# Program order on every engine, paired inverse-RMS chains and step-paced loads in a windowed-attention and feed-forward kernel

## The chip, the cores and the metric

One core of one Trainium2 chip. The metric is device time of one execution in microseconds (us), lower is better. The clock that the throttle grants to the matmul engine is recorded for each run.

Engine names are those of the profile: PE (TensorE, matmul), PEld (its weight loads), DVE (VectorE), ACT (ScalarE), POOL (GpSimd), SP (SyncE, which here only issues DMAs).

## The reference

Two stages, cut to what matters. Attention over 4 batches, 8 heads, 768 tokens, head size 64, where a token sees 128 earlier tokens and the first 4 ("sinks"). Its output, 3072 tokens of 512 values, goes through RMS normalization and a SwiGLU feed-forward network (FFN) with 1536 hidden values.

```python
keep = is_sink | in_window                       # window 128, 4 sinks
a = softmax(where(keep, q @ k.T / 8, -1e9));  x = a @ v        # per head
x = x.transpose(0, 2, 1, 3).reshape(3072, 512)
xn = x / sqrt(mean(x * x) + 1e-6) * rms_g
g = xn @ w_gate
out = (g * sigmoid(g) * (xn @ w_val)) @ w_out
```

## The kernel before

The work is cut into 24 attention blocks of 128 tokens (6 a batch) and 6 FFN groups of 4 blocks (512 tokens). While PE runs the FFN of group G, the attention of the blocks of group G+1 and later is woven in between.

The names that the profile uses: `qs`, `ks`, `v` are loaded blocks; `qkT` the transposed q and k; `pT` scores in PSUM; `et` their exponentials; `pv` attention output with its denominator; `x` the normalized attention output; `sq` and `ms` its squares and their sums; `m`, `y` the inverse-RMS chain; `xr` the RMS-normalized block; `pxt` and `xnt` its transpose in PSUM and SBUF (blocks 8 and later are transposed by DMA); `pg`, `pvl` gate and value matmuls; `th`, `p`, `hT` the three steps of SwiGLU; `po` output matmuls; `osb` their eviction.

The inverse RMS of one block, on DVE, six small dependent operations and then `xr`:

```python
def unit_rms(g):
    x16 = X16.pop(g).rearrange("p h d -> p (h d)")
    ms = MS.pop(g)
    nc.vector.scalar_tensor_tensor(out=m, in0=ms[:, 0:1], scalar=RMS_EPS, in1=ms[:, 1:2], ...)
    nc.vector.tensor_scalar(out=y[:, 0:1].bitcast(I32), in0=m.bitcast(I32), ...)   # first guess
    # ... four more scalar_tensor_tensor on [128, 1] ...
    # unit_xr:
    nc.vector.scalar_tensor_tensor(out=xr, in0=x16, scalar=y[:, 4:5], in1=gb, ...) # times rms_g
```

The FFN is a list of "parts". For each hidden tile `ft` there is a gate part and a value part; for each of the four token blocks three output parts, each of which contracts four of the twelve hidden tiles:

```python
def gate():
    st["pg"] = mms("pg", wg, G, fts, cols)                       # PE, 4 matmuls 128x512
    nc.scalar.activation(out=st["th"], in_=st["pg"], func=Tanh)  # ACT
def val():
    pvl = mms("pvl", wv, G, fts, cols)
    nc.vector.scalar_tensor_tensor(out=p1, in0=st["th"], in1=st["pg"], ...)   # DVE: p
    nc.vector.tensor_tensor(out=HT[...], in0=p1, in1=pvl, op=mult)            # DVE: hT
def part(i):                                                     # output part i of 3
    for ft in range(4 * i, 4 * i + 4):
        nc.tensor.matmul(out=st["po"], lhsT=HT[(G, ft // 2)][...], rhs=wo[:, ft, :], ...)
```

Attention units are put in "slots", four for each step, and `weave` spreads the slots evenly over the parts. Which engines keep this order is said by the schedule context:

```python
MANUAL = {PE, SP}
MANUAL_ALL = MANUAL | {Activation, DVE}
with tc.manual_schedule(engines=MANUAL_ALL):     # start: blocks 0 and 1
    unit_warm(6)                                 # dummy matmuls
    # ...
with tc.manual_schedule(engines=MANUAL):         # main part
    for ft in range(0, FA, 2):                   # FA = 10: five tile pairs in token halves
        fa += parts_f(0, (ft, ft + 1), slice(0, GN // 2))
        fb += parts_f(0, (ft, ft + 1), slice(GN // 2, GN))
    # ...
    for G in range(NG):
        # ... gate/value parts, then the output parts of the group
        weave(parts, slots[n:n1], 1)
```

An engine in the set keeps program order; for the others the scheduler picks the order when the program is built. In the main part of this kernel ACT and DVE are left to the scheduler. The token halves of the first group let its FFN start when only blocks 0 and 1 are ready.

The softmax here doesn't subtract the row's maximum and nothing guards it: scores larger than these inputs give would overflow.

## Time and profile before

| | before |
|---|---|
| median time, three executions | 255.85 us (255.73 to 256.4) |
| PE busy | 240.8 us, 95% |
| first FFN matmul | 19.39 us |
| second group starts | 76.43 us |
| PE waits after the first FFN matmul | nine, 5.7 us together |

The page of the kernel before: busy time by engine, then rows of 40 equal slices of the span, where a digit is the busy share in tenths (`PEclk` is the granted clock in tenths).

```profile
PE 240.8 (95%) x1784; PEld 125.2 (49%) x1784; DVE 175.7 (69%) x465; ACT 141.9 (56%) x320; POOL 94.8 (37%) x127
...
PE   6988899989979999999999999999999999999994
...
DVE  4563897998768999348898277998268991277800
...
PEclk9979999999999999999999999999999999999999
```

PE has nines from about 80 us on; all of its waits but one (0.40 us at 128.6 us) lie in front. Busy times in stretches of 10 us, of the kernel before. The columns are stretch, length, then PE, PEld, DVE, ACT and POOL with instruction counts, granted clock, DMA, GB/s:

```profile
40.00:50.00 10.00, 9.50 (x116) 7.76 (x115) 8.96 (x25) 8.32 (x18) 4.64 (x6) 1.00 1.51 195
50.00:60.00 10.00, 9.02 (x92) 5.50 (x93) 9.71 (x26) 8.51 (x21) 9.76 (x12) 1.00 2.43 156
60.00:70.00 10.00, 9.61 (x106) 5.81 (x106) 7.83 (x26) 9.32 (x23) 9.98 (x12) 1.00 2.32 173
...
140.00:150.00 10.00, 10.00 (x69) 4.78 (x67) 3.92 (x14) 5.25 (x14) 0.00 (x0) 1.00 0.34 92
```

From 40 to 70 us DVE and ACT are nearly as full as PE. Who waited for whom on PE, kernel before (us in total, times, longest):

```profile
PE pg L582 <- ACT xnt L568: 1.8, 2, 1.6
PE pT L405 <- ACT qkT L274: 1.4, 2, 1.0
...
PE pv L439 <- DVE hT L608: 0.4, 1, 0.4
```

This is the end of the second group on DVE, kernel before, in order of time (start, duration, engine, line, operation):

```profile
98.35 0.16 DVE L526 SCALAR_TENSOR_TENSOR y<-y 128x1 f32<-128x1 f32 x1
98.42 0.68 DVE L600 SCALAR_TENSOR_TENSOR p<-th,pg 128x512 bf16<-128x512 bf16 x1
99.02 0.75 DVE L542 SCALAR_TENSOR_TENSOR xr<-x,y,gb 128x512 bf16<-128x512 bf16 x1
99.68 0.68 DVE L608 TENSOR_TENSOR hT<-p,pvl 128x512 bf16<-128x512 bf16 x1
...
101.07 0.69 DVE L608 TENSOR_TENSOR hT<-p,pvl 128x512 bf16<-128x512 bf16 x1
```

### The profile page before, as it was taken

To read this page: it belongs to the slowest core of one execution; us is meant where nothing else is said; L and a number is where in the kernel's file an instruction comes from. 1 tells how busy PE (TensorE), PEld (TensorE's weight loads), DVE (VectorE), ACT (ScalarE), POOL (GpSimd) and SP (SyncE) were. 2 spreads that over 40 slices of the span, in tenths; PEclk is the share of its full clock that TensorE was granted. 3 is DMA by queue.
4 is the path that set the end of the run, shared out by engine and by line. 5 is a ranking of instruction groups with operands and counts; after the bars stand their busy time and mean duration, and the time that the engine had idled before them with its cause. 6 is when DMAs were issued, how large, how long until landed. Compare 5 with 4: busy or idle time off the path is not lost.

```text
span 254.6 us, 4880 instructions
## 1 busy us (share of the span) xinstructions
PE 240.8 (95%) x1784; PEld 125.2 (49%) x1784; DVE 175.7 (69%) x465; ACT 141.9 (56%) x320; POOL 94.8 (37%) x127
## 2 busy tenths in 40 slices
PE   6988899989979999999999999999999999999994
PEld 2536677755534444454454444444444444444441
DVE  4563897998768999348898277998268991277800
ACT  2646678879994565475475366566445341333211
POOL 8986778299987440331231003033121000000000
PEclk9979999999999999999999999999999999999999
DMA  9999999999999999435005328215321101200022
GB/s 130 142 171 190 188 157 189 183 156 155 185 174 168 156 155 118 97 89 147 10 12 64 82 62 147 41 23 64 104 61 45 21 18 63 107 0 0 3 82 82
DMA packets 105849, 25.74 MB, mean 101 GB/s; under 512 B 95073, under 2 KB 102753, under 8 KB 105826
## 3 DMA queue, kind: packets, MB, share of 16 engines
q0 software_dynamic: 80704, 13.90, 70.6%
q1 hardware_dynamic: 24082, 11.28, 20.0%
q10 hardware_dynamic: 1040, 0.26, 0.5%
q8 instruction: 14, 0.23, 0.4%
q14 instruction: 9, 0.07, 0.1%
HBM read 28.31 MB, written 6.29 MB: 136 GB/s over the span
## 4 chain that ended last, share of the span: by engine, by line
PE 68%; DVE 12%; ACT 8%; POOL 4%; DMA 3%; issue 2%; POOLq 0%; DVEq 0%; ACTq 0%
PE po L623 20%; PE pg L582 20%; PE pvl L582 19%; DVE hT L608 3%; DVE p L600 3%; DMA ks<-in_k_dram 3%; PE pT L405 2%; ACT et L414 2%; DVE et L380 2%; ACT sq L495 2%; PE pv L453 2%; PE pv L457 2%; ACT qkT L274 1%; DVE x L485 1%; POOL qs L111 1%
## 5 line engine op out<-in xcount | busy, mean ns | idle before, releaser
L582 PE MATMUL pg<-xnt,wg 128*128 128x512 bf16 (+1 forms) x328 | 74.0, 353 | 2.3 <-ACT xnt L568 1.8
L582 PE MATMUL pvl<-xnt,wv 128*128 128x512 bf16 (+1 forms) x328 | 74.0, 353 | 0.0
L595 ACT ACTIVATE th<-pg 128x512 bf16<-128x512 f32 x72 | 43.2, 600 | 51.2 <-PE pg L582 49.8
L623 PE MATMUL po<-wo,hT 128*128 128x512 bf16 x288 | 64.9, 379 | 0.1
L600 DVE SCALAR_TENSOR_TENSOR p<-th,pg 128x512 bf16<-128x512 bf16 x72 | 49.2, 683 | 18.9 <-ACT th L595 18.9
L608 DVE TENSOR_TENSOR hT<-p,pvl 128x512 bf16<-128x512 bf16 x72 | 49.4, 686 | 5.7 <-PE pvl L582 0.9
L582 PEld LDWEIGHTS <-wg 128*128 128x128 bf16 x328 | 31.4, 98 | 30.9 <-issue 2.7
L582 PEld LDWEIGHTS <-wv 128*128 128x128 bf16 x328 | 31.2, 98 | 28.8 <-issue 0.2
L414 ACT ACTIVATE et<-pT 128x512 bf16<-128x512 f32 x76 | 39.5, 605 | 6.7 <-PE pT L405 6.7
L623 PEld LDWEIGHTS <-hT 128*128 128x128 bf16 x288 | 27.4, 98 | 30.6 <-issue 0.2
L382 POOL TENSOR_SCALAR_AFFINE_SELECT et<-et 128x512 bf16<-128x512 bf16 x20 | 12.6, 637 | 79.7 <-ACT et L414 73.2
L630 ACT ACTIVATE osb<-po 128x512 f32<-128x512 f32 x24 | 14.4, 601 | 27.8 <-PE po L623 25.4
L495 ACT ACTIVATE sq<-x 128x256 bf16<-128x256 bf16 x48 | 20.2, 425 | 7.5 <-DVE x L485 7.1
L111 POOL DMA_DIRECT2D qs<-in_q_dram x23 | 20.9, 907 | 7.0 <-DMA wo<-in_moe_w_out_dram 2.5
L111 POOL DMA_DIRECT2D ks<-in_k_dram x23 | 20.8, 904 | 6.6 <-DMA wo<-in_moe_w_out_dram 2.9
L124 POOL DMA_DIRECT2D v<-in_v_dram x24 | 21.7, 903 | 4.3 <-DMA qs<-in_q_dram 2.7
L485 DVE TENSOR_TENSOR x<-pv,rden 128x256 bf16<-128x256 f32 x48 | 20.0, 422 | 0.9
L380 DVE TENSOR_TENSOR et<-et,masks 128x1024 bf16<-128x1024 bf16 (+1 forms) x22 | 13.9, 636 | 8.5 <-ACT et L414 8.4
L542 DVE SCALAR_TENSOR_TENSOR xr<-x,y,gb 128x512 bf16<-128x512 bf16 (+1 forms) x25 | 18.1, 728 | 0.7
L480 DVE RECIPROCAL rden<-pv 128x4 f32<-128x4 f32 x48 | 7.8, 173 | 10.1 <-PE pv L457 10.0
L405 PE MATMUL pT<-qkT 64*128 64x256 bf16 (+1 forms) x168 | 12.0, 261 | 2.1 <-ACT qkT L274 1.4
L457 PE MATMUL pv<-v,et 128*128 128x65 bf16 x168 | 12.6, 194 | 0.0
(72 smaller groups left out, 198.3 us busy)
## 6 DMA issues: line engine op xcount, KB each, us to landing
out_dram<-osb SPq DMA_DIRECT2D x24, 256.0 KB, 2.2
v<-in_v_dram POOLq DMA_DIRECT2D x24, 128.0 KB, 7.6
qs<-in_q_dram POOLq DMA_DIRECT2D x23, 128.0 KB, 7.5
ks<-in_k_dram POOLq DMA_DIRECT2D x23, 128.0 KB, 7.5
wg<-in_moe_w_gate_dram POOLq DMA_DIRECT2D x6, 256.0 KB, 8.6
wv<-in_moe_w_val_dram POOLq DMA_DIRECT2D x6, 256.0 KB, 8.9
wo<-in_moe_w_out_dram POOLq DMA_DIRECT2D x2, 768.0 KB, 10.7
osb<-in_k_dram ACTq DMA_DIRECT2D x1, 256.0 KB, 4.5
```

Of the source, the lines that this page charges most:

```text
L111: nc.gpsimd.dma_start(out=tl, in_=src[b, :, t * P:(t + 1) * P, :].rearrange("h t d -> t h d"),)
L124: nc.gpsimd.dma_start(out=V16[b][:, t, :, 0:D], in_=v[b, :, t * P:(t + 1) * P, :].rearrange("h t d -> t h d"),)
L380: nc.vector.tensor_tensor(out=e, in0=e, in1=mv, op=ALU.mult)
L414: nc.scalar.activation(out=et[:, hi].rearrange("p j n c -> p (j n c)"), in_=banks[u][hi], func=ACT.Exp, scale=inv_sqrt_d,)
L485: nc.vector.tensor_tensor(out=X16[g][:, heads_of(g, u), :], in0=pvv[:, :, 0:D], in1=RDEN.pop((g, u)).unsqueeze(2).to_broadcast((P, 4, D)), ...
L495: nc.scalar.activation(out=sq, in_=xh, func=ACT.Square, scale=MS_SCALE, accum_out=MS[g][:, u:u + 1],)
L542: nc.vector.scalar_tensor_tensor(out=XR[g][-1], in0=x16[:, c], scalar=y[:, 4:5], in1=gb[:, c], op0=ALU.mult, op1=ALU.mult,)
L582: nc.tensor.matmul(out=ps[:, i * n:(i + 1) * n], lhsT=w_sb[:, kt, ft * P:(ft + 1) * P], rhs=XNT[G][:, kt, cols], start=(kt == 0), stop=(kt ...
L595: nc.scalar.activation(out=st["th"], in_=st["pg"], func=ACT.Tanh, scale=0.5)
L600: nc.vector.scalar_tensor_tensor(out=p1, in0=st["th"], scalar=1.0, in1=st["pg"], op0=ALU.add, op1=ALU.mult,)
L608: nc.vector.tensor_tensor(out=HT[key][:, i:i + n, cols], in0=p1.rearrange("p (n c) -> p n c", n=n), in1=pvl.rearrange("p (n c) -> p n c", ...
L623: nc.tensor.matmul(out=st["po"], lhsT=HT[(G, ft // 2)][:, ft % 2, tb * P:(tb + 1) * P], rhs=wo[:, ft, :], start=(ft == 0), stop=(ft == FTN ...
```

## The change

Its intent: take the scheduler's guesses out of the main part and place everything by hand; save DVE work by sharing one RMS chain between two blocks; start the FFN sooner; and spread the loads so that masks can move to POOL. The diff, cut to its core (cuts marked with `# ...`):

```diff
-    FA = 10
-    POOL_MASK_FROM = 2
-    MANUAL = {mybir.EngineType.PE, mybir.EngineType.SP}
+    FA = 8
+    POOL_MASK_FROM = 1
+    MANUAL = {mybir.EngineType.PE, mybir.EngineType.SP, mybir.EngineType.Pool}
# ... loads: no longer all at once behind the output weights, but by step
+    LOADS = {4: (8, 9), 5: (10, 11), 6: (12,), 7: (13, 14), 8: (15,), ...}
# ... blocks 12 and 18 are transposed by DMA too
-        return g >= DMA_T_FROM and g % NT > 0
+        return g >= DMA_T_FROM
# ... work put off by n parts
+    def later(n, f):
+        if DEFER[0] and n:
+            LATER.append([n, f])
+        else:
+            f()
+    def tick():                       # after each part
+        for e in LATER:
+            e[0] -= 1
+        # ... runs what is due
+            wait = 0 if not dve else 1 if g < GB else 1 + 2 * u      # masks on DVE
+                later(wait, lambda u=u, et=et, his=his: masked(u, et, his))
-            unit_sq(g, u)
-        if u == 1 and g >= 2:
-            unit_rms(g)
+            later(1 if g < GB else 2, lambda: unit_sq(g, u))
+        if u == 1 and g >= 2 and g % 2 == 1:
+            later(2 if g < GB else 4, lambda: unit_rms(g))           # both blocks of a pair
# ... unit_rms: seven operations on [128, 2], then xr of both blocks in a row
+        for i in range(2):
+            unit_xr(g - 1 + i, y[:, 5, i:i + 1])
# ... blocks 0 to 3: xr without rms_g, which the transposed eviction applies
+            nc.vector.tensor_scalar(out=xr, in0=x16, scalar1=y, scalar2=None, op0=ALU.mult)
# ... start: 9 warm-up matmuls, not 6, and others moved
-    with tc.manual_schedule(engines=MANUAL):
+    with tc.manual_schedule(engines=MANUAL_ALL):
+        DEFER[0] = True
+        run(fa, [ ... ])
+        run(fb[:8], [
+            [unit_bias(3, 1), unit_x(2), unit_sp(3, 1), unit_x(3)],
# ...
```

## The prediction

> **What bounds the kernel now.** TensorE (PE). The page gives PE 95% busy, and from 80 us on the timeline shows feed-forward (FFN) matmuls back to back: four 128x512 in 0.86 us. Stretch by stretch, PE is busy 10.0 of 10 us nearly everywhere after 80 us, but 7.5 to 9.6 before. So what can be won lies in the first 80 us:
> - The first FFN matmul starts at 19.39 us.
> - After it the timeline shows nine PE waits, together 5.7 us: 0.74 on ACT qkT, 0.74 on DVE qkT, 0.50 and 0.40 for DVE, 0.98 and 0.39 on ACT qkT, 0.17 and 0.23 around xnt, and 1.59 on ACT xnt before the second FFN group at 76.4. With about 0.17 us of modelled matmul tail before each, my estimate is 7.3 us.
> - From 40 to 70 us DVE is busy 7.8 to 9.7 of 10 us and ACT 8.3 to 9.3; their queues cause those waits.
>
> **What the change does.**
> 1. Two blocks share one inverse-RMS chain. Now each block pays six dependent DVE operations, 13.28 to 14.47 us for the first. Two chains become one of seven (estimate 1.35 us). For the first four blocks the gain moves to the transposed eviction, so xr should cost about 0.3 us (as masks, 128x512, 0.29), not 0.75. Both first xr should be ready at 15.8 us, not 17.1, and no 2.3 us of warm-up matmuls stand between the two transposes. First FFN matmul: about 18.2 us, gain 1.2.
> 2. Blocks 12 and 18 are transposed by DMA: 16 fewer PE transposes, 0.44 us a block, gain 0.9 us of bound PE time.
> 3. Masks of blocks 7 to 11 move from DVE (two of 0.69 us) to POOL (four of 0.64). DVE gets slack. POOL issues loads too (0.9 us each), so it becomes nearly full about 57 to 73 us.
> 4. Program order on ACT, DVE and POOL, with masks, squares and RMS put off by one to four parts, and the last x transposes of the second group placed ahead of four or more output matmuls: this should remove most of the 0.98, 0.50 and 1.59 us waits; gain about 3.2 us after 38 us.
> 5. Four tile pairs in halves, not five: the same matmul time, but the second half of the tokens is needed 1.7 us of PE work earlier. I expect a new wait: the transposes of blocks 2 and 3 stand right before the matmuls that need them, with two exps (1.0 us) between their evictions on ACT. Estimate 2.3 us against 0.75 now, loss 1.5; about 1.2 us is won back before it.
>
> Loads land in about 7.5 us; two blocks ahead should suffice. Nothing changes after 130 us.
>
> **Sum.** 1.2 + 0.9 + 3.2 + 1.2 - 1.5 = 5.0 us; perhaps more, since the tuning removes waits that I only guessed. Predicted 250.6 us, 80% range 247.5 to 253.8. Chances: faster by over 2% 0.50, within 2% 0.47, slower 0.03.
>
> **What would show it.** First FFN matmul near 18.2 us (right) or after 19 (step 1 wrong). DVE below 8 of 10 us in 40 to 70. Second FFN group starting about 72 us with no wait on xnt. A wait of 1 to 2.5 us on xnt or xr near 34 us (step 5). Sixteen fewer 128x128 PE transposes.
>
> **What would make it wrong.** Masks on POOL late behind load issues. ACT blocked at the head of its queue by program order. PE at half speed in the first FFN matmuls: the Trainium skill ("TensorE: Matmul & The Clock Gate", The HAM clock gate) tells of a half-rate clock after low activity; this trace agrees, warm-ups taking 0.47 us each at 16 to 18 us against 0.22 at full speed.

## More of the kernel before

The scheduler threaded an RMS chain between `p` and `hT`, a small operation at a time, and the last `hT` is done at 101.8 us. On PE the output matmuls start at 101.02 us, and the twelfth, the first to need that `hT`, comes over 2 us later, so it doesn't wait:

```profile
101.02 1.89 PE L623 MATMUL po<-wo,hT 128*128 128x512 bf16 x8
...
103.00 3.18 PE L623 MATMUL po<-wo,hT 128*128 128x512 bf16 x14
```

## The result and the profile after

| | before | after |
|---|---|---|
| median time, four executions of each | 255.79 us (255.45 to 256.4) | 264.62 us (264.12 to 267.6) |
| first FFN matmul | 19.39 us | 17.09 us |
| second group starts | 76.43 us | 75.97 us |
| third group starts | 112.99 us | 118.21 us |
| sixth group starts | 219.7 us | 230.3 us |
| span of the profiled run | 254.6 us | 265.6 us |

The ratio is 1.036 (95% interval 1.030 to 1.043): slower, where 0.98 was expected. Ratios here are the mean time of one kernel's fast runs over that of the other's of the same rounds, so they are not quite the ratio of the medians that are quoted. The milestones are those of the profiled runs. After the change the attention work of one step (8 `pT`, 18 `pv` and 4 `pss` matmuls, about 1.3 us of PE time) has moved from before the second group's start to behind it, so 75.97 us is about 0.8 us later than 76.43 us for the same work (estimate). From the third group's start on, both kernels have done the same attention work.

The page of the changed kernel, same rows as before:

```profile
PE 244.9 (92%) x1735; PEld 124.3 (47%) x1761; DVE 167.9 (63%) x398; ACT 139.0 (52%) x322; POOL 106.1 (40%) x145
...
PE   7989879998999996999998998998999998999993
...
DVE  4644757796658988317979139988139984078700
...
PEclk9968979999999999799999999999999999999998
```

DVE has less to do (167.9 against 175.7 us), as intended, and PE is idle more. There are new gaps far behind 80 us, once in each group, and dips of the clock near 18, 37 and 109 us. Stretches of the changed kernel:

```profile
40.00:50.00 10.00, 9.95 (x105) 7.13 (x103) 7.21 (x13) 6.81 (x13) 5.61 (x7) 1.00 1.50 191
...
60.00:70.00 10.00, 8.66 (x86) 4.97 (x86) 5.55 (x18) 9.61 (x25) 9.32 (x12) 1.00 1.24 99
...
100.00:110.00 10.00, 7.58 (x41) 3.24 (x41) 7.59 (x21) 4.20 (x12) 1.86 (x4) 0.86 0.94 82
...
140.00:150.00 10.00, 8.69 (x62) 4.10 (x61) 6.83 (x18) 3.68 (x9) 1.47 (x3) 1.00 0.30 41
```

PE's waits in the changed kernel:

```profile
PE po L669 <- DVE hT L654: 6.0, 4, 2.2
...
PE pg L628 <- ACT xnt L617: 1.2, 1, 1.2
PE pxt L601 <- DVE xr L574: 1.1, 1, 1.1
```

The new first line is the largest. The four waits are at 106.0, 146.3, 185.1 and 222.4 us, one at the end of each group from the second to the fifth. The first of them on PE:

```profile
101.27 2.54 PE L669 MATMUL po<-wo,hT 128*128 128x512 bf16 x11
106.00 0.39 PE L669 MATMUL po<-wo,hT 128*128 128x512 bf16 x1 [2.20 <-DVE hT L654]
```

Eleven output matmuls run, and the twelfth, the one that needs tile 11, waits. On DVE at that time:

```profile
100.69 0.69 DVE L654 TENSOR_TENSOR hT<-p,pvl 128x512 bf16<-128x512 bf16 x1
101.30 0.68 DVE L409 TENSOR_TENSOR et<-et,masks 128x1024 bf16<-128x1024 bf16 x1
101.90 0.15 DVE L541 SCALAR_TENSOR_TENSOR m<-ms 128x2 f32<-128x2 f32 x1
...
103.14 1.42 DVE L578 SCALAR_TENSOR_TENSOR xr<-x,y,gb 128x512 bf16<-128x512 bf16 x2
104.47 0.68 DVE L646 SCALAR_TENSOR_TENSOR p<-th,pg 128x512 bf16<-128x512 bf16 x1
105.26 0.69 DVE L654 TENSOR_TENSOR hT<-p,pvl 128x512 bf16<-128x512 bf16 x1
```

A mask and the whole paired RMS chain with both `xr`, from 101.90 to 104.47 us, stand ahead of the last `p` and `hT`. Nothing needs that `xr` soon: the third group starts at 118 us. The operation that PE needs is last in the queue. The Trainium skill ("TensorE: Matmul & The Clock Gate", Architectural detail) says of the queues that "ACT/DVE are strict FIFO"; this trace agrees: the inputs of the last `p` and `hT` were there by about 101.4 us (ACT's last `th` and PE's last `pvl` matmul are done by then), yet DVE first works off 2.6 us of RMS, and PE stands 2.2 us until the two operations behind it are done.

The wait that the prediction had foreseen where the token halves meet, on PE:

```profile
33.86 0.40 PE L601 MATMUL pxt<-ident,xr 128*128 128x128 bf16 x4 [1.15 <-DVE xr L574]
...
36.10 1.91 PE L628 MATMUL pg<-xnt,wg 128*128 128x256 bf16 x8 [1.17 <-ACT xnt L617]
37.80 1.58 PE L628 MATMUL pvl<-xnt,wv 128*128 128x256 bf16 x8
39.22 1.04 PE L628 MATMUL pg<-xnt,wg 128*128 128x256 bf16 x8
```

1.15 and 1.17 us. After it eight matmuls take 1.70 us to the next group's start (36.10 to 37.80), where they take 0.87 us elsewhere: PE runs at half rate. The granted clock in three stretches of the changed kernel (the clock is the number before the last two):

```profile
14.00:22.00 8.00, 7.14 (x51) 4.48 (x50) 3.09 (x8) 4.00 (x11) 6.17 (x9) 0.57 1.87 179
34.00:40.00 6.00, 4.83 (x40) 3.44 (x39) 3.24 (x7) 2.71 (x7) 5.45 (x7) 0.72 2.49 155
104.00:112.00 8.00, 5.78 (x38) 2.73 (x40) 3.90 (x10) 4.12 (x12) 3.86 (x6) 0.79 0.53 100
```

It is 0.57, 0.72 and 0.79. In the kernel before the same stretches have 0.79, 1.00 and 1.00. Over the runs of the changed kernel the mean clock was 0.993 to 0.972 and the time 264.12 to 267.6 us, in the main the slower the lower, so these dips go with up to 3.5 us from run to run; the best-clocked run is still 8 us over before.

### The profile page after: what moved, and what is told of

Read it like the earlier page. It is cut to its first block, busy times and chain, and to the rows that moved or that the text cites. A ratio compares the mean times of both kernels' runs of the same rounds, so it can differ in the third digit from the quotient of the medians.

```text
span 265.6 us, 4787 instructions
## 1 busy us (share of the span) xinstructions
PE 244.9 (92%) x1735; PEld 124.3 (47%) x1761; DVE 167.9 (63%) x398; ACT 139.0 (52%) x322; POOL 106.1 (40%) x145
## 4 chain that ended last, share of the span: by engine, by line
PE 58%; DVE 28%; ACT 8%; issue 4%; DMA 1%; DVEq 0%; ACTq 0%
PE po L669 17%; PE pg L628 16%; PE pvl L628 15%; DVE hT L654 7%; DVE p L646 6%; DVE xr L578 5%; ACT et L443 2%; PE pT L434 2%; ACT th L641 2%; DVE x L522 2%; PE pqk L241 2%; DVE et L409 2%; DMA osb<-in_q_dram 1%; PE pv L487 1%; PE pv L483 1%
## 5 line engine op out<-in xcount | busy, mean ns | idle before, releaser
L628 PE MATMUL pg<-xnt,wg 128*128 128x512 bf16 (+1 forms) x310 | 75.2, 364 | 3.2 <-ACT xnt L617 1.2
L669 PE MATMUL po<-wo,hT 128*128 128x512 bf16 x279 | 66.5, 385 | 6.6 <-DVE hT L654 6.0
L411 POOL TENSOR_SCALAR_AFFINE_SELECT et<-et 128x512 bf16<-128x512 bf16 x30 | 19.5, 656 | 85.8 <-ACT et L443 77.9
L669 PEld LDWEIGHTS <-hT 128*128 128x128 bf16 x288 | 27.7, 99 | 39.3 <-DVE hT L654 8.0
L517 DVE RECIPROCAL rden<-pv 128x4 f32<-128x4 f32 x48 | 8.4, 176 | 32.5 <-PE pv L487 32.5
L416 POOL TENSOR_SCALAR_AFFINE_SELECT et<-et 128x512 bf16<-128x512 bf16 x24 | 16.0, 667 | 0.0
L578 DVE SCALAR_TENSOR_TENSOR xr<-x,y,gb 128x512 bf16<-128x512 bf16 x20 | 14.9, 785 | 0.4
## 6 DMA issues: line engine op xcount, KB each, us to landing
out_dram<-osb SPq DMA_DIRECT2D x24, 256.0 KB, 2.2
wg<-in_moe_w_gate_dram POOLq DMA_DIRECT2D x6, 256.0 KB, 8.1
wv<-in_moe_w_val_dram POOLq DMA_DIRECT2D x6, 256.0 KB, 8.2
osb<-in_q_dram SPq DMA_DIRECT2D x1, 256.0 KB, 3.9
```

Source lines behind the costliest of these rows:

```text
L411: nc.gpsimd.affine_select(out=ev[:, :, 0, :], in_=ev[:, :, 0, :], compare_op=ALU.is_ge, fill=0.0, base=0, pattern=[[0, x], [1, P]], channe ...
L578: nc.vector.scalar_tensor_tensor(out=xr, in0=x16, scalar=y, in1=gb, op0=ALU.mult, op1=ALU.mult,)
L628: nc.tensor.matmul(out=ps[:, i * n:(i + 1) * n], lhsT=w_sb[:, kt, ft * P:(ft + 1) * P], rhs=XNT[G][:, kt, cols], start=(kt == 0), stop=(kt ...
L669: nc.tensor.matmul(out=st["po"], lhsT=HT[(G, ft // 2)][:, ft % 2, tb * P:(tb + 1) * P], rhs=wo[:, ft, :], start=(ft == 0), stop=(ft == FTN ...
```

## The experiments

Fifteen kernels, all correct. Unless said otherwise a time is the median of all runs (in e1, e2, e12 and e13 one of them is marked slow), and "before" in the same rounds had 255.5 to 256.0 us.

A run is marked slow when it is over 1.5% above the fastest of its kernel; ratios use the other, fast runs alone. Theory A was: program order on DVE (and ACT) in the main part costs the time, because the RMS chain stands ahead of the last `hT`. Rival B: the paced loads and the masks on POOL. Rival C: the half-rate clock.

### e1 and e2: give the order back to the scheduler

```diff
-    with tc.manual_schedule(engines=MANUAL_ALL):      # main part
+    with tc.manual_schedule(engines=MANUAL):          # e1: ACT and DVE free
+    with tc.manual_schedule(engines=MANUAL | {Activation}):   # e2: DVE free
```

> The changed kernel with ScalarE and VectorE left to the scheduler again in the main part, as before; all else of the change stays. Theory A (program order on these two engines lost the time, chiefly the four waits of the output matmuls for hT, 1.25 to 2.2 us each): those four waits go, and the time falls by 6 us or more, to 258 us or less. Rival B (the loads and the masks on GpSimd cost it): the time stays within 2 us of 264.5. Rival C (the half-rate clock after the early start costs it): the time falls by under 3 us.

> Only VectorE is left to the scheduler; ScalarE keeps program order. Theory A with VectorE as the culprit: within 1 us of e1_free, 258 us or less. If program order of ScalarE matters as much: about half of e1_free's gain. Rivals B and C: near 264.5 us.

Measured: e1 268.95 us (ratio 1.050), e2 266.81 us (1.040). Neither gains; e1 is even slower. The waits of `po` for `hT` do shrink (to 1.3 and 1.0 us), but another takes their place. PE's waits in e1:

```profile
PE pg L628 <- ACT xnt L608: 4.7, 1, 4.7
PE pxt L601 <- DVE xr L574: 2.5, 3, 2.1
```

On DVE in e1:

```profile
75.16 0.35 DVE L296 COPY ksk<-qkT 64x16 bf16<-64x16 bf16 x2 [3.32 <-DMA qkT<-ks]
```

The RMS of blocks 6 and 7 is not late: both `xr` are done at 71.8 us and their transposes on PE at 72.3. But `ksk`, DVE's copy of the next batch's sink keys, waits until 75.16 us for a DMA transpose of 6.1 us (block 12, which step 2 of the prediction took off PE). The normalization `x` of the next block stands behind it on DVE, the squares of `x` stand ahead of the last `xnt` on ACT, and the second group starts 4.7 us late (4.2 us in e2, by the same chain). So the blunt form of theory A, "program order is bad here", falls: the scheduler's order of this program is no better. What matters is where single operations stand. That the scheduler would do better with block 12 still transposed on PE was not tried.

### e3: move one pair of operations

From block 8 on the RMS chain is put off by six parts, not four. On DVE this moves only `p` and `hT` of one tile ahead of each chain; PE, ACT and POOL keep the same order instruction for instruction (SP's DMA issues shift with it).

```diff
-            later(2 if g < GB else 4, lambda: unit_rms(g))
+            later(2 if g < GB else 4 if g < DMA_X_FROM else 6, lambda: unit_rms(g))
```

> Program order kept on every engine; from block 8 on the inverse RMS of a pair is put off by six parts, not four, which moves only the last p and hT of each group ahead of it on VectorE (TensorE, ScalarE and GpSimd have the same order). Theory A in its sharp form (the 2.7 us RMS chain ahead of the last hT): the waits of po for hT fall from 6.0 us in total to under 1, and the time falls by about 6 us, with the clock dip near 107 us gone too, to 257 to 259 us. Rival B or C: no change, 264 us.

Measured: 257.66 us (256.76 to 258.28), ratio to before 1.007. Of the 8.8 us, 7.0 us are gone (264.62 less 257.66). The same place on PE in e3:

```profile
100.43 2.75 PE L669 MATMUL po<-wo,hT 128*128 128x512 bf16 x12
103.11 0.61 PE L434 MATMUL pT<-qkT 64*128 64x256 bf16 x8
```

All twelve output matmuls run through. And on DVE in e3:

```profile
101.06 0.68 DVE L646 SCALAR_TENSOR_TENSOR p<-th,pg 128x512 bf16<-128x512 bf16 x1
101.85 0.69 DVE L654 TENSOR_TENSOR hT<-p,pvl 128x512 bf16<-128x512 bf16 x1
102.45 0.15 DVE L541 SCALAR_TENSOR_TENSOR m<-ms 128x2 f32<-128x2 f32 x1
...
103.70 1.42 DVE L578 SCALAR_TENSOR_TENSOR xr<-x,y,gb 128x512 bf16<-128x512 bf16 x2
```

`hT` first, the RMS chain after it. No wait of `po` for `hT` is left, and the clock in the stretch 104 to 112 us is 1.00. The waits were 6.0 us, or 6.7 with about 0.17 us of matmul tail hidden before each (an estimate). The clock has a share in the 7.0 us: runs with the same mean clock took 264.12 us (changed kernel, 0.993) and 258.10 and 258.28 us (e3, 0.992 and 0.993), so about 5.9 us are the order itself and about 1 us goes with the lower clock of the other runs of the change. This is the sharp form of theory A, and it is shown. It also speaks against C as the main cause: in e3's profile the clock dip at 34 to 40 us is still there (0.74).

### e4: program order alone, in the kernel before

```diff
-    with tc.manual_schedule(engines=MANUAL):          # main part of before
+    with tc.manual_schedule(engines=MANUAL_ALL):
```

> The kernel before, with program order on ScalarE and VectorE in the main part and nothing else. If program order as such costs the time, with no deferral to soften it: 262 to 275 us, with waits on hT and on masks. If only the change's own deferral did it: within 2 us of 255.8.

Measured: 275.19 us, ratio 1.075. PE waits for `xnt`, `qkT` and `ksk` again and again up to 90 us, and the second group starts at 88.9 us. Program order without any put-off is worse than the change by 10 us. That the deferral makes this difference is argued, for the change differs from e4 in its start, its paired chains, its loads and its masks too.

### e7: the old loads and masks (rival B)

On top of e3, all loads at once behind the output weights, and masks of blocks 7 to 11 back on DVE.

```diff
-    POOL_MASK_FROM = 1
+    POOL_MASK_FROM = 2
-        load_q(2 * GB)
-    LOADS = {4: (8, 9), 5: (10, 11), ...}
+    LOADS = {}
+        for g in range(2 * GB, NB):       # ahead of the main part
+            unit_load(g)
```

> e3_rms_late with the loads and the masks of the kernel before: all loads issued at once after the output weights, masks of blocks 7 to 11 on VectorE. Rival B (the new loads and masks cost time): the time falls by over 2 us, to 255.5 or less. If they help, as the prediction said, by unloading VectorE: the time rises, by 1 to 6 us. If they don't matter: 257 to 258.5.

Measured: 256.71 us (255.89 to 257.17), ratio 1.004 against e3's 1.007, with overlapping intervals. That is below the 257 to 258.5 us expected if they don't matter and above the 255.5 of rival B, and within the noise of e3. Rival B falls as the cause of the 8.8 us, and so does my hope that they help: loads and masks together are worth nothing that shows (e11 against e10, below, says the same).

### e5 and e8: undo the four-pair split, first try

Five pairs again, and the transposes of blocks 2 and 3 one part ahead of their reader. e5 on top of e3, e8 on the changed kernel as it is.

```diff
-    FA = 8
+    FA = 10
-        run(fa, [
+        run(fa[:8], [
# ... in run(fb[:8], ...) the first slot becomes empty
-            [unit_bias(3, 1), unit_x(2), unit_sp(3, 1), unit_x(3)],
+        run(fa[8:], [
+            [],
+            [unit_bias(3, 1), unit_x(2), unit_sp(3, 1), unit_x(3)],
```

> e3_rms_late plus the undoing of the four-pair split: five tile pairs in halves again, and the transposes of blocks 2 and 3 one part ahead of the first matmul that needs them. If step 5 of the prediction is right (the split costs a wait of 1.1 us on xr and 1.2 us on xnt near 32 to 34 us, and the half-rate clock that follows it costs some 1.5 us more): those waits fall below 0.5 us together, the clock dip at 34 to 37 us goes, and the time falls by 2.5 to 3.5 us from 257.7, to 254 to 255. If the split is innocent: 257 to 258 us.

> The changed kernel with only that last edit (five pairs, transposes one part earlier), the RMS chain left where the change put it. If the two causes add: 264.6 less about 3, so 261 to 262 us, with the four waits for hT still there (5 to 7 us in total). If the time gained in front only lengthens the waits for hT: 263.5 us or more.

Measured: e5: three of its four runs were marked slow (its profiled run had a clock of 0.842 and took 292 us), and the one fast run took 260.98 us. e8: 274.26 us, ratio 1.073, 10 us slower than the change. The two waits where the halves meet did fall, from 1.15 and 1.17 to 0.58 and 0.20 us. PE's largest waits in e8:

```profile
PE pxt L601 <- DVE xr L578: 8.1, 2, 4.4
PE po L669 <- DVE hT L654: 6.0, 4, 2.2
```

The edit had a flaw. The rest of the first group now has 18 parts, not 20, for the same slots, so fewer parts lie between an attention block and the transposes of its pair. The chains of blocks 4 and 5 and of blocks 6 and 7, put off by four parts, came to stand right ahead of their readers. A delay counted in parts is tied to how many parts a group has. A second thing made it worse. The first operation of the chain on DVE in e8:

```profile
57.41 2.65 DVE L541 SCALAR_TENSOR_TENSOR m<-ms 128x2 f32<-128x2 f32 x1
```

Where no mask ran on POOL at the time, it took 0.15 to 0.16 us. Here four masks ran back to back on POOL from 57.65 to 60.04 us, and it ended at 60.06.

### e6: e5 with two more edits

In each step the transposes of a coming block ahead of the x transposes, and the second mask one part sooner.

```diff
-            wait = 0 if not dve else 1 if g < GB else 1 + 2 * u
+            wait = 0 if not dve else 1 if g < GB else 1 + u
# step(): slots[1].append(unit_t(g + 2)) now comes before unit_x
```

> e5_fa10, and in each step the transposes of a coming block issued ahead of the x transposes (against the 1.0 us wait of the sink scores on ScalarE's qkT near 63 us and the 0.4 us on xnt before the second group), and the second mask of a block one part earlier. If the remaining loss is these waits: 252 to 253.5 us, faster than before by about 1%. If VectorE has no room in the first 100 us: within 1 us of e5_fa10.

Measured: 264.87 us, ratio 1.035. The 1.0 us wait of the sink scores is gone, but it carries the flaw of e5 (waits of 2.9 and 3.8 us for `xr`), so as an attempt at a better kernel it says little.

### e9, e10 and e11: the same without the flaw

```diff
-            later(1 if g < GB else 2, lambda: unit_sq(g, u))
-            later(2 if g < GB else 4 if g < DMA_X_FROM else 6, lambda: unit_rms(g))
+            later(1 if g < DMA_X_FROM else 2, lambda: unit_sq(g, u))
+            later(2 if g < DMA_X_FROM else 6, lambda: unit_rms(g))
# e10: e9, and unit_t(g + 2) before unit_x within a step
# e11: e10, and loads and masks as in e7
```

> e5_fa10 again without its flaw: the parts of the first group got fewer, so a delay counted in parts put the RMS chain of blocks 4 to 7 right before its reader; here squares and RMS of these blocks are put off by one and two parts, not two and four. If the four-pair split and that flaw are separate causes: no wait on xr above 0.5 us at blocks 4 and 6, and 253.5 to 255.5 us, some 3 us under e3_rms_late. If five pairs do not fit program order at all: 258 us or more.

> e9_fa10_soon with the transposes of a coming block ahead of the x transposes within a step. If the 1.0 us wait of the sink scores on ScalarE's qkT near 62 us still binds, it goes and the time falls by about 1 us; if it has slack already, no change within 0.7 us.

> e10_tfirst with the loads and masks of the kernel before. e7_old_loads was 1 us under e3_rms_late, within the noise of either. If that was real: 1 us under e10_tfirst, and about 252 to 254 us, below the kernel before by 0.5 to 1.5%. If it was noise, or VectorE has less room here: equal to e10_tfirst or up to 2 us above.

Measured: e9 256.54 us (ratio 1.003), e10 257.03 (1.004), e11 256.98 (1.005). e9 is 1.1 us under e3, not 3. The waits where the halves meet are 0.28 and 0.20 us, down from 2.3, and the clock stays at 1.00 from 20 to 110 us; but a wait of 1.88 us appears at 57 us, attention on the mask of block 6, and 0.74 us on `xr` at 69 us. In e10 and e11 the sink scores no longer wait, and DVE's masks cost PE 3.2 and 4.5 us (2.6 in e9). Much of what one edit wins in the first group, the next wait in it takes back, but not all. The profiled runs show where the rest goes. In e9 the second group starts at 72.68 us, 3.75 us before that of the kernel before; 1.3 us of this is the work moved behind it, so about 2.4 us are won (estimate). The second group then takes 38.80 us against 36.56, with the moved work and with waits of 0.49 and 0.33 us for `hT` and `p` at 93 us. The fourth takes 37.81 us against 36.62, with waits of 0.40 and 0.78 us near 158 us. PE's last matmul ends only 0.6 us earlier than before.

### e12, e13 and e14: what is left

```diff
# e12: e9, DVE free in the main part
# e13: e9, both masks of blocks 4 to 6 put off by one part
-            wait = 0 if not dve else 1 if g < GB else 1 + 2 * u
+            wait = 0 if not dve else 1 if g < DMA_X_FROM else 1 + 2 * u
# e14: e13, and from block 8 on the two xr each a part later than the chain
-            unit_xr(g - 1 + i, y[:, 5, i:i + 1])
+            later(0 if g < DMA_X_FROM else 1 + i,
+                  lambda i=i: unit_xr(g - 1 + i, y[:, 5, i:i + 1]))
```

> e9_fa10_soon with VectorE left to the scheduler in the main part. If program order on VectorE is what keeps the repaired change above the kernel before: the waits on hT, p and et after 90 us go and the time falls to 253 to 255. If the scheduler's order is no better for this program, as e1 and e2 (269 and 267 us) suggest: 258 us or more, with a new wait on xr or xnt before the second group.

> e9_fa10_soon with both masks of blocks 4 to 6 put off by one part instead of one and three. If the late second mask is a cause of its own: the wait of the attention matmuls on et near 57 us (1.9 us) goes and the time falls by 1 to 2 us, to 254.5 to 255.5. If VectorE merely passes the delay on (to xr, hT or rden): within 0.7 us of e9's 256.5.

> e13_mask_soon with the RMS chain of blocks 8 on cut in three on VectorE: the chain, then one xr, then the other, each a part later, so that no block of 2.7 us stands in VectorE's queue. If long solid blocks in an in-order queue are the cause of what remains after 75 us (waits on p and hT of 0.3 to 0.8 us, two or three in a group): those waits at least halve and the time falls by 1 to 2 us under e13, to 253 to 254.5, below the kernel before. If not: equal to e13.

Measured: e12 268.96 us (1.049), with one wait of 5.6 us for `xr` at 74 us. As in e1, `ksk` stands waiting for the DMA transpose of block 12 (until 71.64 us), this time in the middle of the RMS chain. e13 257.81 us (254.95 to 259.5; ratio 1.003, interval 0.998 to 1.009): the wait at 57 us is gone, and 1.2 us for `ksk` has come (POOL's mask costs 0.7 us, 0.6 in e9); no change that shows. e14 256.19 us (1.002, interval 0.997 to 1.007): of the waits after 75 us three of 0.33, 0.61 and 0.80 us are left, 1.7 us against e13's 2.5, so they did not halve, and the time is that of before within the noise.

### e15: the new start alone, in the kernel before

The kernel before with the change's start and nothing else: one chain for blocks 0 and 1, `rms_g` applied at the transposed eviction, the new warm-up.

```diff
-        unit_warm(6)
+        unit_warm(9)
# ... prologue in the order of the change, with
-        unit_rms(0); unit_xr(0); unit_rms(1); unit_xr(1)
+        unit_rms01()                      # seven operations on [128, 2], xr by tensor_scalar
# main part as before, scheduler on ACT and DVE
```

> The kernel before with only the change's start: one RMS chain for blocks 0 and 1, their gain in the transposed eviction, the new warm-up and prologue order. The main part keeps the scheduler on VectorE and ScalarE, a chain for each block, the old loads and the split in five pairs. If step 1 of the prediction carries to the end: the first feed-forward matmul near 17.2 us, not 19.4, and 253.5 to 254.5 us, about 0.8% faster than before. If ScalarE and VectorE between 20 and 76 us set the pace and not the start: the lead is gone by the second group (76.4 us) and the time is within 0.7 us of before.

Measured: 256.10 us (255.26 to 256.78), ratio 1.001 (0.998 to 1.003). The first FFN matmul comes at 16.99 us, 2.4 us earlier than before, and nothing is gained. PE in e15:

```profile
16.99 1.87 PE L626 MATMUL pg<-xnt,wg 128*128 128x256 bf16 x8 [0.61 <-DVE qkT L260]
...
22.93 0.61 PE L413 MATMUL pT<-qkT 64*128 64x256 bf16 x8 [0.67 <-ACT qkT L260]
...
54.65 0.61 PE L413 MATMUL pT<-qkT 64*128 64x256 bf16 x8 [0.97 <-ACT qkT L282]
```

The same scores start at 23.61 us in the kernel before, so by 22.93 us only 0.7 us of the lead is left; in this run half rate had taken the rest. By 54.65 us (before: 54.70) all of it is gone, at a wait for ACT's `qkT`, and the second group starts at 76.39 us (before: 76.43). The runs of e15 with a clock of 0.997 or 0.998 took 255.3 to 255.8 us, so with hardly a dip the lead is lost as well. Between 20 and 76 us not PE's start but the chains over ACT and DVE set the pace. The chain of work that ended last, which the profile follows back from the end, taken from 39.3 to 76.4 us in e15, is 17.2 us of DVE, 14.5 of ACT and 2.9 of PE, the rest short pauses, and nearly the same in the kernel before. POOL and the DMAs are not on it, though POOL was busy 9.76 and 9.98 of 10 us from 50 to 70 us. So neither DVE nor ACT alone sets the pace: the chain runs over both in turn.

## Why the prediction was wrong

Predicted 250.6 us (247.5 to 253.8), measured 264.62 us. A gain of 5 us was forecast and a loss of 8.8 us came.

- **The step that failed is step 4**, "Program order on ACT, DVE and POOL, with masks, squares and RMS put off by one to four parts", to which I gave 3.2 us of gain, together with the sentence "Nothing changes after 130 us". I had looked for DVE's order only where PE had been waiting before. The put-off of four parts places the paired chain ahead of the last `p` and `hT` of each group, where the scheduler had kept `hT` in time. Four waits of 1.25 to 2.20 us followed, three of them after 130 us. e3 moves one `p` and `hT` ahead of each chain and wins 7.0 us. Of the waits that step 4 was to remove, that for `xnt` before the second group did shrink, from 1.59 to 0.41 us, but waits of 0.58 us (a mask, at 50.6 us) and 1.04 us (ACT's `qkT`, at 65.3 us) stand where 0.50 and 0.98 us stood, and the second group started at 75.97 us, not 72.
- **Step 1 was right in its mechanism and its gain was more than I said**: the first FFN matmul at 17.09 us, not 18.2. But I booked the lead as time won at the end. e15 shows that it is worth nothing in the kernel before: half rate and the chains over ACT and DVE have taken it back by 55 us. The error is one of bookkeeping across stages: a lead on PE is a gain only if PE sets the pace from there on.
- **Step 2 was right**: the trace shows 96 `pqk` transposes, 112 before. Its 0.9 us can't be told apart from the rest.
- **Step 3 was half right**: from 40 to 70 us DVE is busy 7.21, 9.20 and 5.55 of 10 us against 8.96, 9.71 and 7.83, not below 8 throughout. POOL, said to become nearly full from 57 to 73 us, was busy 13.5 of these 16 us, less than the 15.3 before. But e7 shows that loads and masks are worth nothing here. One cost was overlooked: masks on POOL hold up DVE. In the changed kernel's chain of blocks 6 and 7, the operations from 69.36 to 70.91 us took 0.35, 0.55, 0.54 and 0.55 us while POOL's masks ran, against 0.15 to 0.17 us otherwise; in e7, with these masks on DVE, the same chain's operations took 0.15 to 0.29 us.
- **Step 5 was right in place and size**: waits of 1.15 and 1.17 us at 34 to 36 us, 2.3 us as predicted. What came on top is the half rate after it, 0.8 and 0.6 us in the first two parts. e9 took most of these waits away and won only 1.1 us over e3, with new waits in their place.
- **The risks**: of those named, half rate came true. The same instructions, from the first FFN matmul to the next q transpose, took 5.05 us in the profiled run of the changed kernel and 2.88 us in that of e3, whose code is the same up to there. The Trainium skill ("TensorE: Matmul & The Clock Gate", The HAM clock gate) says that the activity window is free-running, so that the same kernel differs from run to run; this agrees. It fits the spread of the runs.

What stays open: the repaired change (e9, e14) has less DVE work, fewer transposes and an earlier start, and is still not under the kernel before. e15 shows that the start doesn't count in the kernel before, e7 that loads and masks don't. In the profiled run of e9 some 2.4 us are won in the first group and most of it is lost in the second and fourth, at short waits for `hT`, `p` and `et`; that removing those would bring the gain home is argued, for e14 removed part of them and shows no gain beyond the noise. No version ran faster than the kernel before beyond the noise.

## What to carry to other kernels

When a kernel goes from a scheduler to program order, look at the end of every stage: name the operation that the next stage's first blocked instruction needs, and see what stands ahead of it in its engine's queue; work that is needed much later, such as the next group's normalization, belongs behind it. The same holds for an operation that will have to wait, such as `ksk` for its DMA: all that stands behind it waits too. That merging two short chains into one long block makes such a misplacement dearer is likely (2.6 us here against 1.9 us for the single chain before) but was not tested alone. A delay counted in steps of the program changes its meaning when the number of steps does, and a lead won on one engine at the start is worth something only after the stage that follows has been shown to be bound by that engine.

## What the Trainium skill lacked or had wrong

- "TensorE: Matmul & The Clock Gate", The HAM clock gate, names an idle window of about 3.4 us as what takes the clock down. Here PE went to half rate after less: after one wait of 2.2 us at 106 us (clock 0.79 over 104 to 112 us), and after two waits of 1.15 and 1.17 us within 4 us (0.72 over 34 to 40 us). Single waits of 1.25 to 1.27 us, at 146, 185 and 222 us, were not followed by a dip (clock 1.00 in those stretches). The length of a wait alone does not decide: in e4 a wait of 2.06 us that ended at 69.1 us was followed by a dip (0.57 over 70 to 74 us), and one of 2.94 us that ended at 36.9 us was not (1.00 from 33 to 45 us).
- The same page, same section, puts the cost of the ramp at the start below 1% of a typical span. The runs don't contradict that, but with dips in the middle of the kernel as well, runs of one kernel lay 1.3% apart, from 264.12 us (mean clock 0.993) to 267.6 us (0.972).
- No page has the rule that mattered most here: that in an in-order queue a late-needed block of 2.6 us in front of two operations of 0.7 us cost PE 1.25 to 2.2 us in each of four groups, 6.0 us of waits in all.
